# Feed-forward tiles of 512 columns in pairs whose matmuls take turns

## The chip, the cores and the metric

The kernel runs on one core of a Trainium2 chip. The metric is the device time in microseconds (us) of one execution. A core has a matrix engine (TensorE, in the profile PE for the matmuls and PEld for the loads of their stationary operand), a vector engine (VectorE, DVE), a scalar engine (ScalarE, ACT), GpSimd (POOL), and queues that issue DMAs (SyncE, SP). TensorE writes its results to PSUM, which has eight banks; one bank holds a tile of 128 partitions by 512 columns in float32. VectorE and ScalarE read the tiles from there.

## The reference

Attention with a sigmoid in the place of the softmax, for 8 batches of 12 heads, 448 positions and 64 channels, and on its output a gated feed-forward layer without bias:

```python
scores = scale * np.matmul(q, k.transpose(0, 1, 3, 2)) - np.log(S)
attn = 1.0 / (1.0 + np.exp(-scores))
attn_out = np.matmul(attn, v)                     # (8, 12, 448, 64)
x = attn_out.transpose(0, 2, 1, 3).reshape(3584, 768)
gate = 1.0 / (1.0 + np.exp(-(x @ w_gate)))        # 768 -> 1536
val = x @ w_val                                   # 768 -> 1536
out = gate * val @ w_out                          # 1536 -> 768
```

## The kernel before, in words

The attention part comes first and fills the first 258 us. Its matmuls (L225 and L244) are not touched. Then two feed-forward stages follow: gate and value in the first, the output projection in the second. Both compute transposed: output channels on the partitions, tokens along the columns.

The 3584 tokens are seven tiles of 512 columns. Six of them are taken in three sets of two (PAIR), and each such set is multiplied by a Strassen-like scheme with seven block products (`SETS`, index i from 0 to 6), with sums of weight blocks and of token blocks prepared beforehand. The seventh tile is the set ALONE, with four products. So a stage has the sets PAIR, ALONE, PAIR, PAIR, with 7, 4, 7 and 7 products; one product is called a round here.

Every float32 operand is split in two parts, a high one (the value rounded to the matmul's format) and a low one (the rest). A product of two blocks of 128 is three matmuls, low weight by high data, high by low, high by high, all added into one accumulator in PSUM. The function `product` (L403) issues them: for each of three blocks of the contraction three matmuls, nine in all, one after the other into the same accumulator `acc`. Each matmul has 128x128 weights and 512 columns, so an accumulator fills a bank.

**First stage** (loops at L469 to L560): three passes over the weights, in each the four sets, in each set its rounds r, and in each round four output tiles q, two of the gate and two of the value in turns (q even: gate, q odd: value). Per q: nine matmuls, then the reading of the accumulator (ScalarE copies for i = 0 and takes the sigmoid; VectorE adds or multiplies for the others), then `tick()` (L530), which issues what fell due (stores of results, splits of later weights), and then by q the splits of coming operands: `high_x` on ScalarE after q = 1, `low_x` on VectorE after q = 2 (with the load of a later operand), and steps that prepare the later weights on VectorE and GpSimd (L554 to L558).

**Second stage** (loops at L576 to L635): the same four sets and their rounds, in each round two halves of the contraction, and in each half three output tiles o. Per half and o again nine matmuls; an accumulator collects both halves and is read after the second (`evacuate`, L583). `high_h` and `low_h` split the coming operands, one per half.

`starts` (L400) says in which rounds a tile begins a new accumulator: rounds 0, 2 and 5 of PAIR, 0 and 2 of ALONE. `bank()` (L397) then hands out the next of the eight banks. In the other rounds the nine matmuls add onto what the same bank already holds, also where it has been read in between: such a tile is read after round 0 and added to in round 1, read after 2 and added to in 3, and so on.

The order of all work is written out by hand: each engine takes its instructions in the order in which the program issues them, and the framework adds the waits between engines, here above all that a matmul which adds to a bank waits for the read before it, and that a read waits for the last matmul before it.

Of the kernel before, what the change touches and what calls it, by code (L numbers as in the profile page):

```python
# [39 lines left out]
def sigmoid_attention_glu_kernel(ctx: ExitStack, tc: tile.TileContext, qk, v, wg, wv, wo, out):  # L40
    nc = tc.nc
# [8 lines left out]
    HC = NC // 2  # L50
# [5 lines left out]
    NQUAD = 2 * JS  # L56
# [22 lines left out]
    def tick(flush=False):  # L79
        clock[0] += 1  # L80
        due = [e for e in later if e[0] <= clock[0] or flush and e[2]]
        later[:] = [e for e in later if e not in due]
        for _, fn, _ in due:
            fn()

    def new_w(i):
        return keep.tile([P, NQUAD, 2, HW], F32R, tag=f"w{i}", name=f"w{i}")

    W = [new_w(i) for i in range(NP)]
# [79 lines left out]
    x_loaded, ops = {}, {}  # L169
# [25 lines left out]
    with tc.tile_pool(name="att", bufs=2) as att, tc.tile_pool(name="sc", bufs=2, space=PSUM) as scp, \  # L195
# [157 lines left out]
        for cols in (S, S // 2):  # L353
            for h in range(2):
                for u in range(2):
                    nc.tensor.matmul(sc[halves[u], h, :cols], lhsT=zeros[halves[h]], rhs=zeros[halves[h], :1].broadcast_to([HP, cols]),
                                     start=True, stop=True)
        beats, beat, done = B * NQ * 7, 0, 0
        for m in range(B * NQ):
            for g in range(7):  # L360
# [21 lines left out]
                if beats - 7 < beat < beats - 3:  # L382
                    k = beat - beats + 6
# [11 lines left out]
    with tc.tile_pool(name="mm", bufs=8, space=PSUM, reuse_waits="tile") as mm:  # L395

        def bank():  # L397
            return mm.tile([P, F], F32, tag="mm", name="acc")

        def starts(p, n):  # L400
            return n in (0, 2, 5) if SETS[p] is PAIR else n in (0, 2)

        def product(acc, pairs, first, half=None):  # L403
            terms = []
            for w, x, k in pairs:
                terms += [(w[:, 1, k[0]], x[:, 0, k[1]]), (w[:, 0, k[0]], x[:, 1, k[1]]), (w[:, 0, k[0]], x[:, 0, k[1]])]
            for n, (a, b) in enumerate(terms):
                nc.tensor.matmul(acc, lhsT=a, rhs=b, start=first and n == 0 and half != 1, stop=n == len(terms) - 1 and half != 0,  # L408
                                 skip_group_check=not first)

        def cols(k):
            return slice(k * P, (k + 1) * P)

        def add(o, a, b):
            nc.vector.tensor_tensor(out=o, in0=a, in1=b, op=ALU.add)  # L415
# [5 lines left out]
        o_order = [(p, k, h) for p in range(NSET) for _, k in SETS[p] for h in range(2)]  # L421
        h_loaded, h_ops, wx = {}, {}, {}

        def load_h(m):
            if m < len(o_order):
                p, i, h = o_order[m]
                h_loaded[m] = src_tile() if m < 4 or h == 0 else fo.tile([P, 3, F], F32, tag="src2", name="src2", bufs=2)
                nc.sync.dma_start(out=h_loaded[m], in_=h_src[p][i][h])

        def high_h(m):  # L430
            if m < len(o_order):
                h_ops[m] = op_tile() if m % 4 < 3 else fo.tile([P, 2, 3, F], F32R, tag="op2", name="op2", bufs=1)
                high(h_ops[m], h_loaded[m])

        def low_h(m):
            if m < len(o_order):
                low(h_ops[m], h_loaded.pop(m))
# [17 lines left out]
        with tc.tile_pool(name="ff", bufs=1, reuse_waits="tile") as ff:  # L455
# [6 lines left out]
            n = 0  # L462
# [6 lines left out]
            for s in range(NPASS):  # L469
                for p in range(NSET):  # L470
                    st = [{} for _ in range(NQUAD)]
# [3 lines left out]
                    for r, (i, _) in enumerate(SETS[p]):  # L475
                        for q in range(NQUAD):
                            d, t, jl = st[q], q % 2, q // 2
                            j = s * JS + jl
                            gate = st[q - 1] if t else None
                            if starts(p, r):  # L480
                                d["acc"] = bank()
                            acc = d["acc"]
                            product(acc, [(W[i][:, q], ops[n], (cols(k), k)) for k in range(HC)], starts(p, r))
                            if SETS[p] is ALONE:
                                if r % 2 == 0:
                                    pass
# [21 lines left out]
                            elif i in (2, 3):  # L508
                                k = "u2" if i == 2 else "u3"
                                d[k] = unit(k, 4)  # L510
                                add(d[k], acc, d["s1"])
                            else:
                                k, to = {4: ("s1", 1), 5: ("u3", 6), 6: ("u2", None)}[i]
# [55 lines left out]
        with tc.tile_pool(name="fo", bufs=1, reuse_waits="tile") as fo:  # L569
            def unit2(tag):  # L570
                return fo.tile([P, F], F32, tag=tag, name=tag, bufs=3)

            tick(flush=True)
            load_h(5)
            m = 0
            for p in range(NSET):  # L576
                st = [{} for _ in range(HC)]

                def save(o, b, y, queue=nc.sync, a=slice(0, F)):
                    t = (BLOCK[p] + b) * F  # L580
                    queue.dma_start(out=out[o, :, t + a.start:t + a.stop], in_=y[:, a])

                def evacuate(r, i, o, d, acc):  # L583
                    if SETS[p] is ALONE:
                        if r % 2:
                            y = unit2("c11" if r == 1 else "s1")
                            nc.scalar.copy(y, acc)
                            save(o + r // 2 * HC, 0, y)
                    elif i == 0:
                        d["s1"] = unit2("s1")  # L590
                        nc.scalar.copy(d["s1"], acc)
                    elif i == 1:
                        y = unit2("c11")
                        nc.scalar.copy(y, acc)
                        save(o, 0, y)
                    elif i in (2, 3):
                        k = "u2" if i == 2 else "u3"
                        d[k] = unit2(k)
                        add(d[k], acc, d["s1"])
                    else:  # L600
                        k, mo, b = {4: ("s1", HC, 0), 5: ("u3", HC, 1), 6: ("u2", 0, 1)}[i]
                        if m + 2 < len(o_order) or o < HC - 1:
                            add(d[k], acc, d[k])
                            save(o + mo, b, d[k])
                        else:
                            for queue, a in ((nc.scalar, slice(0, F // 2)), (nc.sync, slice(F // 2, F))):
                                add(d[k][:, a], acc[:, a], d[k][:, a])
                                save(o + mo, b, d[k], queue, a)

                for r, (i, _) in enumerate(SETS[p]):  # L610
                    for half in range(2):
                        for o in range(HC):
                            d = st[o]
                            if half == 0 and starts(p, r):
                                d["acc"] = bank()
                            js = range(3 * half, 3 * half + 3)
                            product(d["acc"], [(W[i][:, j] if j < NQUAD else wx[i][:, j - NQUAD], h_ops[m + half], (cols(o), j % 3)) for j in js], starts(p, r), half)
                            if half == 1:
                                evacuate(r, i, o, d, d["acc"])
                            tick()  # L620
                            if (half, o) == (0, 0) and m > 0:
                                high_h(m + 2)
                            if (half, o) == (0, 1) and m > 0:
                                low_h(m + 2)
                                load_h(m + 6)
                            if (half, o) == (1, 1):
                                high_h(m + 3)
                            if (half, o) == (1, 2):
                                low_h(m + 3)
                                load_h(m + 7 if m > 0 else 6)  # L630
                                if m == 0:
                                    load_h(7)
                    h_ops.pop(m)
                    h_ops.pop(m + 1)
                    m += 2  # L635
# [39 lines left out]
```

## Time and profile before

| | |
|---|---|
| runs | 1180.48, 1181.24, 1181.71 us (median 1181.24) |
| profiled execution | 1181.84 us, its span 1180.0 us |
| attention, by TensorE | up to 258.2 us |
| feed-forward stages, by TensorE | 918.26 us, 4050 matmuls |
| of these the first stage | 75 rounds of 36 matmuls |
| and the second | 25 rounds of 54 matmuls |
| granted TensorE clock | 1.000 |

The page gives the busy time of each engine, the span in 40 slices, the DMA queues, the chain of work that ended last, and the costliest groups of instructions. A row of the timeline has the start and the length in us from the span's start, the engine, the line, the operation, out<-in by tile names, shapes, and the number of instructions that were merged; in brackets stands the idle time of the engine before it and what ended that. A matmul's row is longer than the distance to the next one, since matmuls overlap. In the second stage weights with j below 4 are in a tile named w, the others in wr, wf or wsum.

### The profile page before, as it was taken

Reading aid. Unit: us, or ns where it says so; the run is one execution under the profiler, and the core shown is the slowest. Engines: PE = TensorE matmul, PEld = TensorE weight load, DVE = VectorE, ACT = ScalarE, POOL = GpSimd, SP = SyncE. Lnnn points to the kernel's source line nnn. Section 1 sums busy time; section 2 is a strip of 40 time slices with the busy share of each in tenths; the row PEclk is TensorE's granted clock in tenths of the full one; section 3 lists DMA queues with packets and bytes.
Section 4 is the critical chain, followed back from the end, with each engine's and each line's share of the span. In section 5 each row is a group of like instructions: output and inputs, shape, how many; then the busy total and the mean of one; then the engine's idle time right before and its main releaser. Section 6 shows DMA issues by size and latency. Waiting matters only on the chain.

```text
span 1180.0 us, 17018 instructions
## 1 busy us (share of the span) xinstructions
PE 1175.3 (100%) x6754; PEld 858.2 (73%) x6754; DVE 698.6 (59%) x725; ACT 488.6 (41%) x516; POOL 301.6 (26%) x232
## 2 busy tenths in 40 slices
PE   9999999999999999999999999999999999999998
PEld 3333333348888888888888888888888888888887
DVE  3334334326898658889965888657685542334343
ACT  6777777772232325322233532324344212422320
POOL 1325225161362413146340425405020000000000
PEclk9999999999999999999999999999999999999999
DMA  7588866867798576759967666746786453445531
GB/s 295 164 249 279 287 222 224 310 233 263 237 322 297 195 250 222 262 181 334 309 204 271 226 213 230 260 158 200 277 278 242 164 198 141 156 154 182 176 110 72
DMA packets 105520, 266.95 MB, mean 226 GB/s; under 512 B 19936, under 2 KB 54880, under 8 KB 105440
## 3 DMA queue, kind: packets, MB, share of 16 engines
q1 hardware_dynamic: 105296, 265.73, 65.8%
q8 instruction: 53, 0.87, 0.3%
q14 instruction: 27, 0.22, 0.1%
q10 hardware_dynamic: 144, 0.13, 0.0%
HBM read 178.91 MB, written 86.90 MB: 225 GB/s over the span
## 4 chain that ended last, share of the span: by engine, by line
PE 99%; DMA 0%; DVE 0%; DVEq 0%; issue 0%
PE acc L408 78%; PE sc L225 11%; PE av L244 11%; DMA qk<-qk 0%; PE av L225 0%; DVE u L415 0%; DVEq L669 0%
## 5 line engine op out<-in xcount | busy, mean ns | idle before, releaser
L408 PE MATMUL acc<-op,w 128*128 128x512 f32 x3600 | 828.3, 389 | 0.0
L408 PEld LDWEIGHTS acc<-op,w 128*128 128x128 f32 x3600 | 675.8, 188 | 140.8 <-issue 0.7
L181 DVE TENSOR_TENSOR op<-src,op 128x1536 fp32r<-128x1536 f32 x125 | 233.7, 1880 | 107.6 <-ACT op L178 57.4
L178 ACT CAST op<-src 128x1536 fp32r<-128x1536 f32 x124 | 183.1, 1479 | 188.8 <-PE acc L408 173.5
L228 ACT ACTIVATE a<-sc,bias 128x896 f32<-128x896 f32 x167 | 168.2, 1007 | 64.5 <-PE sc L225 60.7
L225 PE MATMUL sc<-qk 64*64 64x448 f32 x1336 | 155.5, 541 | 0.2 <-DMA qk<-qk 0.2
L244 PE MATMUL av<-a,v 64*64 64x448 f32 x1344 | 154.7, 536 | 0.0
L415 DVE TENSOR_TENSOR u<-acc,s 128x512 f32<-128x512 f32 x90 | 61.6, 687 | 76.5 <-PE acc L408 76.4
L225 PEld LDWEIGHTS sc<-qk 64*64 64x64 f32 x1336 | 48.3, 134 | 78.4 <-issue 65.7
L244 PEld LDWEIGHTS av<-a,v 64*64 64x64 f32 x1344 | 48.3, 133 | 78.1 <-issue 77.4
L527 POOL TENSOR_TENSOR t<-u,v 128x512 f32<-128x512 f32 x17 | 32.4, 1905 | 279.9 <-DVE u L418 230.2
L415 DVE TENSOR_TENSOR u<-acc,u 128x512 f32<-128x512 f32 (+1 forms) x91 | 61.7, 681 | 63.0 <-PE acc L408 62.8
L142 POOL TENSOR_TENSOR wsum<-wf 128x384 f32<-128x384 f32 x18 | 23.2, 1291 | 209.4 <-DVE wf L130 208.5
L520 ACT ACTIVATE u<-u 128x512 f32<-128x512 f32 x36 | 22.8, 633 | 92.0 <-DVE u L415 87.8
L520 ACT ACTIVATE s<-s 128x512 f32<-128x512 f32 x18 | 11.4, 632 | 102.5 <-DVE s L415 102.5
L415 DVE TENSOR_TENSOR s<-acc,s 128x512 f32<-128x512 f32 x45 | 31.0, 688 | 35.3 <-PE acc L408 35.2
L408 PE MATMUL acc<-op,wr 128*128 128x512 f32 x198 | 50.2, 389 | 0.0
L314 DVE TENSOR_TENSOR op<-av,op 128x448 f32<-128x448 f32 x24 | 15.0, 624 | 58.6 <-ACT op L268 58.6
L314 DVE TENSOR_TENSOR x<-av,x 128x448 f32<-128x448 f32 x24 | 15.0, 624 | 51.1 <-ACT x L268 50.8
L408 PEld LDWEIGHTS acc<-op,wr 128*128 128x128 f32 x198 | 37.2, 188 | 7.7
L130 DVE SCALAR_TENSOR_TENSOR wf<-wr,wf 128x768 uint32<-128x768 uint32 x36 | 41.9, 1164 | 0.7
L443 DVE TENSOR_TENSOR w<-w 128x1536 fp32r<-128x1536 f32 x21 | 41.1, 1959 | 0.0
(62 smaller groups left out, 709.0 us busy)
## 6 DMA issues: line engine op xcount, KB each, us to landing
src<-xs SPq DMA_DIRECT2D x75, 768.0 KB, 4.9
src<-hs SPq DMA_DIRECT2D x50, 768.0 KB, 5.3
qk<-qk SPq DMA_DIRECT2D x23, 896.0 KB, 5.0
hs<-t SPq DMA_DIRECT2D x78, 256.0 KB, 5.8
w<-ws SPq DMA_DIRECT2D x14, 768.0 KB, 6.6
v<-vv SPq DMA_DIRECT2D x23, 448.0 KB, 4.6
wr<-wg SPq DMA_DIRECT2D x12, 768.0 KB, 6.8
wr<-wv SPq DMA_DIRECT2D x12, 768.0 KB, 6.6
```

The costliest lines, as they stand in the source:

```text
L130: nc.vector.scalar_tensor_tensor(out=a, in0=raw[:, :, 0], scalar=29, in1=a, op0=ALU.logical_shift_right, op1=ALU.bitwise_or)
L178: nc.scalar.copy(op[:, 0], src)
L181: nc.vector.tensor_tensor(out=op[:, 1], in0=src, in1=op[:, 0].bitcast(F32), op=ALU.subtract)
L225: nc.tensor.matmul(sc[halves[u], h, :S], lhsT=qkt[halves[h], p, k0:k0 + HP], rhs=qkt[halves[h], p, :S], start=True, stop=True)
L228: nc.scalar.activation(a, sc[:, :, :S], AF.Sigmoid, bias=bias, scale=scale)
L244: nc.tensor.matmul(avs[key][halves[h], :S], lhsT=vt[halves[u], g, h], rhs=a[halves[u], h], start=start, stop=g == last)
L314: nc.vector.tensor_tensor(out=x, in0=other, in1=x, op=ALU.add)
L408: nc.tensor.matmul(acc, lhsT=a, rhs=b, start=first and n == 0 and half != 1, stop=n == len(terms) - 1 and half != 0, skip_group_check=not ...
L415: nc.vector.tensor_tensor(out=o, in0=a, in1=b, op=ALU.add)
L443: nc.vector.tensor_tensor(out=w[:, :, 1], in0=w[:, :, 1].bitcast(F32), in1=w[:, :, 0].bitcast(F32), op=ALU.subtract)
L520: nc.scalar.activation(d[k], d[k], AF.Sigmoid)
L527: nc.gpsimd.tensor_tensor(out=o, in0=a, in1=b, op=ALU.subtract)
```

## The change

`product`, which issues the matmuls of one tile, becomes `products`, which takes a list of tiles and issues the first matmul of each, then the second of each, and so on. In the first stage it is called at q = 0 and q = 2 with the tiles (q, q + 1), whose banks are taken there, and nothing is issued at q = 1 and q = 3. In the second stage the six groups of a round, numbered e = 3 half + o, are taken in the pairs (0, 1), (2, 3), (4, 5); the pair (2, 3) is half 0 of o = 2 with half 1 of o = 0. The very last round of the second stage keeps its order tile by tile. Reads of accumulators, ticks, splits, loads and stores stay where they were in the program.

```diff
-        def product(acc, pairs, first, half=None):
-            terms = []
-            for w, x, k in pairs:
-                terms += [(w[:, 1, k[0]], x[:, 0, k[1]]), (w[:, 0, k[0]], x[:, 1, k[1]]), (w[:, 0, k[0]], x[:, 0, k[1]])]
-            for n, (a, b) in enumerate(terms):
-                nc.tensor.matmul(acc, lhsT=a, rhs=b, start=first and n == 0 and half != 1, stop=n == len(terms) - 1 and half != 0,
-                                 skip_group_check=not first)
+        def products(tiles):
+
+            terms = [[] for _ in tiles]
+            for t, (_, pairs, _, _) in zip(terms, tiles):
+                for w, x, k in pairs:
+                    t += [(w[:, 1, k[0]], x[:, 0, k[1]]), (w[:, 0, k[0]], x[:, 1, k[1]]), (w[:, 0, k[0]], x[:, 0, k[1]])]
+            last = len(terms[0]) - 1
+            for n in range(last + 1):
+                for t, (acc, _, first, half) in zip(terms, tiles):
+                    nc.tensor.matmul(acc, lhsT=t[n][0], rhs=t[n][1], start=first and n == 0 and half != 1, stop=n == last and half != 0,
+                                     skip_group_check=not first)
...
-                            if starts(p, r):
-                                d["acc"] = bank()
+                            if q % 2 == 0:
+                                for w in (q, q + 1):
+                                    if starts(p, r):
+                                        st[w]["acc"] = bank()
+                                products([(st[w]["acc"], [(W[i][:, w], ops[n], (cols(k), k)) for k in range(HC)], starts(p, r), None) for w in (q, q + 1)])
                             acc = d["acc"]
-                            product(acc, [(W[i][:, q], ops[n], (cols(k), k)) for k in range(HC)], starts(p, r))
...
-                            if half == 0 and starts(p, r):
-                                d["acc"] = bank()
-                            js = range(3 * half, 3 * half + 3)
-                            product(d["acc"], [(W[i][:, j] if j < NQUAD else wx[i][:, j - NQUAD], h_ops[m + half], (cols(o), j % 3)) for j in js], starts(p, r), half)
+                            e = half * HC + o
+                            turn = (e,) if m + 2 == len(o_order) else (e, e + 1) if e % 2 == 0 else ()
+                            tiles = []
+                            for hh, oo in (divmod(w, HC) for w in turn):
+                                if hh == 0 and starts(p, r):
+                                    st[oo]["acc"] = bank()
+                                js = range(3 * hh, 3 * hh + 3)
+                                tiles.append((st[oo]["acc"], [(W[i][:, j] if j < NQUAD else wx[i][:, j - NQUAD], h_ops[m + hh], (cols(oo), j % 3)) for j in js], starts(p, r), hh))
+                            if tiles:
+                                products(tiles)
                             if half == 1:
                                 evacuate(r, i, o, d, d["acc"])
```

## The prediction

> **What bounds the kernel now.** I read the page's shares first, then the chain of waits, then who makes TensorE wait, and last single matmuls in the timeline.
>
> ```profile
> span 1180.0 us, 17018 instructions
> PE 1175.3 (100%) x6754; PEld 858.2 (73%) x6754; DVE 698.6 (59%) x725; ACT 488.6 (41%) x516; POOL 301.6 (26%) x232
> PE 99%; DMA 0%; DVE 0%; DVEq 0%; issue 0%
> ```
>
> The chain in order of time, its last pieces:
>
> ```profile
> 255.94 2.25 PE av L244 x24
> 258.20 918.26 PE acc L408 x4050
> ```
>
> The waits of TensorE over the whole span, longest first, and the matmul line with its duration (min/median/max):
>
> ```profile
> PE sc L356 <- DVE bias L66: 1.0, 1, 1.0
> PE sc L225 <- DMA qk<-qk: 0.2, 1, 0.2
> ...
> L408 PE MATMUL acc<-op,w x3600: 387/389/497, 258.1 to 1174.7; 128*128 128x512 f32 x190
> ```
>
> TensorE's own stream sets the end. The feed-forward matmuls, which the change reorders, are one unbroken piece: 4050 in 918.26 us, 226.7 ns from start to start, and none waits. So the change gains only if that step shrinks, and loses by every wait it lets into the stream. The profiled execution took 1181.84 us, 1.84 around its span; the median of the runs is 1181.24, so I add differences to that.
>
> **Does a change of bank shorten the step?** The kernel before already changes bank after every nine matmuls, so the trace holds the answer. In the output stage the timeline separates matmuls by their weight tile: in the second half of an output tile three read w, then six read wr, and the next w belongs to the next accumulator.
>
> ```profile
> 877.08 1.52 PE L408 MATMUL acc<-op,wr 128*128 128x512 f32 x6
> 878.44 0.84 PE L408 MATMUL acc<-op,w 128*128 128x512 f32 x3
> 879.12 1.52 PE L408 MATMUL acc<-op,wr 128*128 128x512 f32 x6
> 880.48 0.84 PE L408 MATMUL acc<-op,w 128*128 128x512 f32 x3
> ...
> 882.52 1.75 PE L408 MATMUL acc<-op,w 128*128 128x512 f32 x7
> 901.56 1.52 PE L408 MATMUL acc<-op,wr 128*128 128x512 f32 x6
> 902.92 0.84 PE L408 MATMUL acc<-op,w 128*128 128x512 f32 x3
> ...
> 907.00 6.96 PE L408 MATMUL acc<-op,w 128*128 128x512 f32 x30
> ```
>
> And the sixth wr matmul alone, the last write to its bank, from narrow windows of the same timeline:
>
> ```profile
> 878.21 0.39 PE L408 MATMUL acc<-op,wr 128*128 128x512 f32 x1
> 880.25 0.39 PE L408 MATMUL acc<-op,wr 128*128 128x512 f32 x1
> 882.29 0.39 PE L408 MATMUL acc<-op,wr 128*128 128x512 f32 x1
> 902.69 0.39 PE L408 MATMUL acc<-op,wr 128*128 128x512 f32 x1
> 906.77 0.39 PE L408 MATMUL acc<-op,wr 128*128 128x512 f32 x1
> ```
>
> Inside a bank five steps take 878.21 - 877.08 = 1.13 us, 0.226 each. Across a bank 878.44 - 878.21 = 0.23, and 0.23 in the other four pairs too (880.48, 882.52, 902.92, 907.00). Had each bank change saved 10 ns, these would read 0.22 or 0.21. I take the gain per turn as nothing; the rows' rounding leaves some 3 ns either way, which I keep for the rival.
>
> The Trainium skill, "TensorE: Matmul & The Clock Gate", section "Back-to-back issue gap", gives N/2.4 + 2.5 ns for a warm matmul: an estimated 215.8 ns at 512 columns, so by that page this stream has 10.9 ns too much in every step. Were that excess the price of staying in one bank, the some 3550 steps that newly change bank would save an estimated 39 us; the trace disagrees with the figure (226.7), and its bank changes cost the same 0.23.
>
> **What the turns move in the first feed-forward stage.** No matmul, weight load or DMA is added or removed, and the program order on ScalarE, VectorE, GpSimd and the queues stays. What moves is when an accumulator is finished and when its bank is written again. Number the matmuls of a round (one i) from 0. Before, tile q owns 9q to 9q+8. After, tiles 0 and 1 share 0 to 17 and end at 16 and 17; tiles 2 and 3 end at 34 and 35. So tiles 0 and 2 are read 8 steps, 1.81 us, later. Where the next round accumulates into the same bank, its first write used to come 28 steps after the last one; now it comes 20 steps after. A reader has about 4.3 us, less its own latency, where it had 6.1. Ahead of tile 3's read VectorE has tile 2's read, the 1.75 us split of an operand (L181), and in some rounds a weight step. The tightest case is the round that starts at 568.3 (258.13, first row below, + 38 rounds of 36 x 0.2267), where VectorE runs behind:
>
> ```profile
> 258.13 4.17 PE L408 MATMUL acc<-op,w 128*128 128x512 f32 x17
> ...
> 572.78 0.68 DVE L415 TENSOR_TENSOR u<-acc,s 128x512 f32<-128x512 f32 x1
> 573.38 0.94 DVE L128 SCALAR_TENSOR_TENSOR wf<-wr,wf 128x768 uint32<-128x768 uint32 x1
> 574.24 1.28 DVE L415 TENSOR_TENSOR u<-acc,s 128x512 f32<-128x512 f32 x2
> 575.44 1.75 DVE L181 TENSOR_TENSOR op<-src,op 128x1536 fp32r<-128x1536 f32 x1
> 577.11 0.95 DVE L130 SCALAR_TENSOR_TENSOR wf<-wr,wf 128x768 uint32<-128x768 uint32 x1
> 577.98 1.48 DVE L415 TENSOR_TENSOR u<-acc,s 128x512 f32<-128x512 f32 x2
> ```
>
> After the change tile 2 is finished by matmul 34 (576.06); a reader starts 0.43 later (measured below), so 576.49 to 577.17; by the row-to-row steps L181 follows to 578.84, L130 to 579.70, tile 3's read from 579.62 to 580.30. Tile 3 is written again by matmul 55 counted from this round's start, whose weights load as 54 starts, at 580.59. So 0.27 us is left and TensorE does not wait; without a weight step about 1.1 us is left. Cost taken: nothing. If VectorE's split stretched, as it did at the stage's start (second row below, 2.61 for 1.75), some three rounds as tight as this one would lose up to 0.6 us each, 1.8 in all.
>
> ```profile
> 258.84 0.62 DVE L314 TENSOR_TENSOR x<-av,x 128x448 f32<-128x448 f32 x1 [2.18 <-ACT x L268]
> ...
> 260.22 2.61 DVE L181 TENSOR_TENSOR op<-src,op 128x1536 fp32r<-128x1536 f32 x1 [0.75 <-ACT op L178]
> ```
>
> The very first pair writes its second bank 8 steps earlier, at 258.35 instead of 260.17, while the attention's last tiles are still being read. The first accumulator starts at 258.13 under the same reads, so I take nothing; the bound is the 1.1 us until VectorE's last such read ends, 258.84 + 0.62 in the row above.
>
> **What the turns move in the output stage: here a wait comes in.** A round has 54 matmuls, six groups of nine: half 0 of o = 0, 1, 2, then half 1. The pairs are (half 0: o 0, o 1), (half 0: o 2; half 1: o 0), (half 1: o 1, o 2). So o = 1 ends at matmul 52, and the next round's first pair begins with o = 0 at 54 and o = 1 at 55. Before, o = 1 ended at 44 and was next written at 63. Where the next round accumulates into the bank that `evacuate` has just to read, matmul 55 must wait for that read. The reads and their start after the last write:
>
> ```profile
> 903.12 0.69 DVE L415 TENSOR_TENSOR u<-acc,s 128x512 f32<-128x512 f32 x1 [4.39 <-PE acc L408]
> 905.16 0.69 DVE L415 TENSOR_TENSOR u<-acc,s 128x512 f32<-128x512 f32 x1 [1.35 <-PE acc L408]
> 905.77 1.75 DVE L443 TENSOR_TENSOR w<-w 128x1536 fp32r<-128x1536 f32 x1
> 907.44 0.68 DVE L415 TENSOR_TENSOR u<-acc,s 128x512 f32<-128x512 f32 x1
> 908.04 3.41 DVE L181 TENSOR_TENSOR op<-src,op 128x1536 fp32r<-128x1536 f32 x2
> ...
> 880.73 0.59 ACT L591 COPY s<-acc 128x512 f32<-128x512 f32 x1 [1.50 <-PE acc L408]
> ```
>
> The weight loads of the same stretch, and a release from VectorE to another engine:
>
> ```profile
> 878.22 0.64 PEld L408 LDWEIGHTS acc<-op,w 128*128 128x128 f32 x3
> ...
> 301.93 0.68 DVE L415 TENSOR_TENSOR u<-acc,u 128x512 f32<-128x512 f32 x1
> 302.64 0.63 ACT L520 ACTIVATE u<-u 128x512 f32<-128x512 f32 x1 [3.03 <-DVE u L415]
> ```
>
> A read starts 903.12 - 902.69 = 0.43 us after its last matmul starts; VectorE then needs 0.69, ScalarE 0.59; the next engine starts 302.64 - 302.61 = 0.03 later; a weight load leads its matmul by 878.44 - 878.22 = 0.22. For the round that ends at 907.00: matmul 52 starts at 906.54, VectorE reads from 906.97 to 907.66, releases at 907.69. Matmul 55 is due at 907.23, its weight load at 907.01. Held at the weight load, the stream slips 907.69 - 907.01 = 0.68 us; with ScalarE as reader 0.58. Nothing stands ahead of these reads: both engines sat idle before them (1.35, 1.50).
>
> Where the release finds the weights already loaded, only the matmul waits: 0.46 and 0.36. The Trainium skill, "TensorE: Matmul & The Clock Gate", section "Step-by-step: what each phase is for", has weight loads pulled ahead of matmuls in flight, and by that rule it would be these smaller figures. In the trace a load runs one matmul ahead and no further; I take the larger.
>
> How often: a PAIR set reads and goes on accumulating at four joints of rounds: 0 to 1 (ScalarE), 2 to 3, 3 to 4 and 5 to 6 (VectorE). ALONE has none, as its banks are read only in rounds after which new banks start. Three PAIR sets make 12; the very last round runs tile by tile, so o = 1 comes back only at matmul 63 there, which leaves 11: 3 by ScalarE, 8 by VectorE. Sum: 8 x 0.68 + 3 x 0.58 = 7.2 us; with the weights ahead 8 x 0.46 + 3 x 0.36 = 4.8. If a halted stream restarts as slowly as its first matmul (497 ns against 389), 11 x 0.11 = 1.2 more.
>
> The second operand half is needed at matmul 19 of a round instead of 27. Its low part follows both reads and, in five rounds by the code's delays, L443: by the rows 906.97, + 0.61, + 1.67, + 0.60, + 1.75 = 911.60, against a need at 907.00 + 20 x 0.2267 + 0.68 of slip = 912.2. It fits; where no slip precedes it lacks about 0.1 us, once. The end of the kernel is the unchanged single-tile round.
>
> Sum: 0 (banks) + 0 (first stage) + 7.2 + 0.1: **1181.2 + 7.3 = 1188.5 us**, 0.6% slower.
>
> **Rivals.** *The bank matters after all*, by something these bank changes do not show, such as an effect of a whole stream that alternates. It decides from 7.3 us / 3550 = 2 ns per step; at 10 ns it gives 1188.5 - 35.5 = 1153. For it: the step's 226.7 is not explained. Against it: five changes at 0.23. Chance 4%. *The wait does not bite*: the readers finish in time or matmul 55 goes ahead, 1181.3 us. Against it: a read of 0.69 us stands in a gap of three steps, 0.68, and starts 0.43 into it. Chance 8%. *VectorE becomes late in the first stage too*: 1188.5 + 1.8, and with the slow restart 1191.5. For it: 0.27 us of slack in a busy round; against it: 1.1 in the plain ones. Chance 10%. The forecast keeps 78%.
>
> **Range.** From the low side of the waits, 1181.2 + 4.8 = 1186, one lower for the runs' spread (1180.48 to 1181.71), to 1188.5 + 1.8 + 1.2 and 0.5 of the spread, 1192. What lies outside is the first two rivals and little more. A measurement of this kernel tells about 0.2%, 2.4 us: slower 0.88, same 0.08, faster 0.04.
>
> **What would show it.** In the profile after: TensorE's waits list VectorE's L415 (eight) and ScalarE's copies (three) with 0.5 to 0.7 us each, all in the output stage at the start of a round; the step inside stays 0.227; the first stage shows no wait. A step near 0.216, or no such waits, makes the forecast wrong; waits between 260 and 870 us make the third rival right.

## The result

The kernel after takes 1189.39 us (median; 1188.19 to 1189.80) against 1180.86 of the kernel before: 1.0068 of it, with a 95% interval of 1.0055 to 1.0080. It is slower by 0.7%; 1188.5 was forecast, in a range of 1185 to 1192. The 1180.86 is the median of four runs; the longer series of the kernel before beside the experiments have 1181.15 to 1181.57. The profiled execution took 1189.41 us with a span of 1187.6.

The page of the kernel after, its span, shares and chain (line 412 is now the matmul line, L419 the adding read of an accumulator, L597 ScalarE's copying one, L447 the split of later weights on VectorE):

```profile
span 1187.6 us, 17017 instructions
PE 1179.1 (99%) x6754; PEld 856.8 (72%) x6754; DVE 696.9 (59%) x725; ACT 485.0 (41%) x516; POOL 303.6 (26%) x232
...
PE 92%; issue 4%; DMA 1%; DVE 1%; POOL 1%; POOLq 0%; SPq 0%; ACT 0%; DVEq 0%; ACTq 0%
```

The same instructions do the same work; but the chain, which was TensorE for 99%, now leaves TensorE and comes back. (The 4% of "issue" are mostly one piece of 44.5 us from 826.44, where the chain goes from a halt back over VectorE, a DMA and GpSimd; TensorE was busy for 44.26 us of it, so it is no loss of that size.) Its last pieces in order of time (start, length, number of matmuls) show where:

```profile
888.53 19.81 PE acc L412 x86
909.11 12.10 PE acc L412 x52
921.98 24.38 PE acc L412 x106
947.13 73.30 PE acc L412 x322
1021.13 24.34 PE acc L412 x106
1046.24 12.10 PE acc L412 x52
1059.11 24.34 PE acc L412 x106
1084.22 24.34 PE acc L412 x106
1109.22 24.36 PE acc L412 x106
1134.35 12.10 PE acc L412 x52
1147.21 36.84 PE acc L412 x161
```

What was one piece of 4050 matmuls is cut at the joints of rounds: 52 is a round of 54 less two, 106 two rounds less two. Who was waited for, first by the matmuls and then by the weight loads (us in total, times, longest):

```profile
PE acc L412 <- DVE u L419: 2.9, 9, 0.3
...
PE acc L412 <- ACT s L597: 0.8, 3, 0.3
```

```profile
PEld acc L412 <- DVE u L419: 6.4, 9, 0.8
...
PEld acc L412 <- ACT s L597: 2.0, 3, 0.7
PEld acc L412 <- issue: 1.3, 2, 0.7
...
PEld acc L412 <- DVE op L181: 0.6, 2, 0.5
```

The kernel before had only the issue row for its feed-forward loads, 0.7 once. Three waits on ScalarE's copies are there, and nine on VectorE's reads: eight are the forecast joints, the ninth lies in the first stage, near 862 us, right behind the second of the issue rows (0.6 us): two halts in a row. One joint close up, the round that ends near 908.4 (timeline; in brackets the idle time ahead):

```profile
908.17 0.19 PEld L412 LDWEIGHTS acc<-op,w 128*128 128x128 f32 x1
908.37 0.69 DVE L419 TENSOR_TENSOR u<-acc,s 128x512 f32<-128x512 f32 x1 [3.16 <-PE acc L412]
908.39 0.39 PE L412 MATMUL acc<-op,w 128*128 128x512 f32 x1
...
908.97 1.75 DVE L447 TENSOR_TENSOR w<-w 128x1536 fp32r<-128x1536 f32 x1
909.11 3.50 PEld L412 LDWEIGHTS acc<-op,w 128*128 128x128 f32 x16 [0.75 <-DVE u L419]
909.11 3.70 PE L412 MATMUL acc<-op,w 128*128 128x512 f32 x15 [0.33 <-DVE u L419]
```

Matmul 54 goes at 908.39, and with it the weight load of 55 was due. VectorE's read of o = 1 ends at 908.37 + 0.69 = 909.06, and the load starts at 909.11.

Did the turns shorten the step? Matmuls within 500 us of the first stage, from the windows view of the kernel before and then of the kernel after:

```profile
300.00:800.00 500.00, 500.00 (x2207) 414.17 (x2206) 394.51 (x394) 163.42 (x172) 178.69 (x106) 1.00 0.71 245
```

```profile
300.00:800.00 500.00, 500.00 (x2208) 414.29 (x2207) 393.05 (x393) 161.03 (x172) 179.33 (x106) 1.00 0.71 244
```

2207 matmuls with a bank change at one step in nine, 2208 with a bank change at every step (inside a pair, and from one pair to the next). One count is the edge of a window; the step is 226.7 ns in both. A bank that changes is worth nothing here.

### The profile page after: what moved, and what is told of

Its sections match the earlier page's. It is cut to its first block, busy times and chain, and to the rows that moved or that the text cites. A ratio compares the mean times of both kernels' runs of the same rounds, so it can differ in the third digit from the quotient of the medians.

```text
span 1187.6 us, 17017 instructions
## 1 busy us (share of the span) xinstructions
PE 1179.1 (99%) x6754; PEld 856.8 (72%) x6754; DVE 696.9 (59%) x725; ACT 485.0 (41%) x516; POOL 303.6 (26%) x232
## 4 chain that ended last, share of the span: by engine, by line
PE 92%; issue 4%; DMA 1%; DVE 1%; POOL 1%; POOLq 0%; SPq 0%; ACT 0%; DVEq 0%; ACTq 0%
PE acc L412 71%; PE sc L225 11%; PE av L244 11%; DMA hs<-t 1%; DVE u L419 1%; POOL t L533 1%; DVE op L181 0%; DMA qk<-qk 0%; POOLq L681 0%; DVE w L447 0%; ACT s L597 0%; SPq L464 0%; PE av L225 0%; SPq L450 0%; DVEq L681 0%
## 5 line engine op out<-in xcount | busy, mean ns | idle before, releaser
L412 PE MATMUL acc<-op,w 128*128 128x512 f32 x3600 | 848.2, 390 | 3.7 <-DVE u L419 2.9
L181 DVE TENSOR_TENSOR op<-src,op 128x1536 fp32r<-128x1536 f32 x125 | 235.8, 1897 | 109.0 <-ACT op L178 106.9
L419 DVE TENSOR_TENSOR u<-acc,s 128x512 f32<-128x512 f32 x90 | 60.3, 686 | 86.8 <-PE acc L412 86.8
L419 DVE TENSOR_TENSOR u<-acc,u 128x512 f32<-128x512 f32 (+1 forms) x91 | 60.0, 680 | 64.8 <-PE acc L412 64.7
L412 PE MATMUL acc<-op,wr 128*128 128x512 f32 x198 | 57.4, 390 | 0.0
L419 DVE TENSOR_TENSOR s<-acc,s 128x512 f32<-128x512 f32 x45 | 30.0, 686 | 34.9 <-PE acc L412 34.8
L447 DVE TENSOR_TENSOR w<-w 128x1536 fp32r<-128x1536 f32 x21 | 41.1, 1958 | 0.0
```

The lines of the kernel that those rows point to most:

```text
L181: nc.vector.tensor_tensor(out=op[:, 1], in0=src, in1=op[:, 0].bitcast(F32), op=ALU.subtract)
L412: nc.tensor.matmul(acc, lhsT=t[n][0], rhs=t[n][1], start=first and n == 0 and half != 1, stop=n == last and half != 0, skip_group_check=no ...
L447: nc.vector.tensor_tensor(out=w[:, :, 1], in0=w[:, :, 1].bitcast(F32), in1=w[:, :, 0].bitcast(F32), op=ALU.subtract)
```

## The experiments

All times stand against the kernel before, run beside them: 1181.57 us for the first four experiments, 1181.15 for the others but one, where it is given. A slip is the time by which a halt sets the matmul stream back. It is worked out from the matmuls' starts in the trace: the halted step and the next one, less two steps of 0.227 (for the two halts in a row near 862 us four steps, less four).

**The change in the first stage alone.**

```diff
-turn = (e,) if m + 2 == len(o_order) else (e, e + 1) if e % 2 == 0 else ()
+turn = (e,)
```

> The change in the first stage alone; the output stage runs tile by tile as before. Wait theory (the loss is the wait of matmul 55 for the read of o = 1, in the output stage): about 0.8 us over before, all of it the one halt that the changed kernel's trace shows at 862 us, where VectorE reads two tiles late; 1181.7. Rival (taking turns itself costs, spread over all steps of both stages): two thirds of the 8 us, since two thirds of the matmuls lie here: 1186.

Measured: 1181.88 us against 1181.57, ratio 1.0005 (0.9996 to 1.0015). In its trace the output stage has no halt, and the first stage has the one near 862, 0.76 us. The loss does not come from taking turns as such.

**The change in the output stage alone** (the first stage calls `products` with one tile at a time).

```diff
-if q % 2 == 0:
-    for w in (q, q + 1):
-        ...
-    products([... for w in (q, q + 1)])
+if starts(p, r):
+    d["acc"] = bank()
+products([(d["acc"], [(W[i][:, q], ops[n], (cols(k), k)) for k in range(HC)], starts(p, r), None)])
```

> The change in the output stage alone. Wait theory: 11 halts of 0.54 (after ScalarE) and 0.60 us (after VectorE), 6.4 together, one more of 0.3 us for the low part of an operand and some 0.3 that the trace leaves unplaced: 7.1 us over before, 1188.0. Rival (turns cost per step): one third of the 8 us, 1183.6.

Measured: 1188.63 us, ratio 1.0058 (1.0043 to 1.0073), 7.1 us more. The waits of its weight loads:

```profile
PEld acc L412 <- DVE u L419: 6.0, 8, 0.8
...
PEld acc L412 <- ACT s L595: 2.0, 3, 0.7
...
PEld acc L412 <- issue: 0.7, 1, 0.7
...
PEld acc L412 <- DVE op L181: 0.2, 1, 0.2
```

Eight and three, the joints counted ahead of the run. The further halt of 0.3 us for the low part of an operand did not come: of such waits only one is left, 0.15 us of a weight load, which sets the stream back by 0.05. In the trace the matmul stream is 6.8 us longer than before: 6.4 in the eleven halts, 0.4 in the steps behind them (see the sum below). A third of the matmuls carries nearly all of the loss.

**The bank needed one step sooner.** The output stage alone again, with o = 1 ahead of o = 0 in the first pair of a round.

```diff
-turn = ... else (e, e + 1) if e % 2 == 0 else ()
+turn = ... else (e + 1, e) if e == 0 else (e, e + 1) if e % 2 == 0 else ()
```

> Output stage alone, pairs as in the change, but in the first pair of a round o = 1 goes ahead of o = 0, so its bank is written again at matmul 54, one step sooner. Wait theory: each of the 11 halts grows by one step, 0.227 us: 2.5 us more than with the change in the output stage alone, 1190.5. Rival (turns cost per step): no difference from the run with the change in the output stage alone.

Measured: 1191.03 us, ratio 1.0082 (1.0065 to 1.0098), 2.4 us over the run before it, where 2.5 was expected; the matmul streams of the two traces differ by 2.8 us. The joint that was shown above, in this run (TensorE sat idle for 0.33 us there, for 0.65 here):

```profile
907.72 4.57 PE L412 MATMUL acc<-op,w 128*128 128x512 f32 x19 [0.65 <-DVE u L419]
```

A halt after ScalarE slips 0.77 us in place of 0.54, one after VectorE 0.89 in place of 0.60: a step or a little more each. No matmul, pair or count of turns differs between the two; only the distance from a bank's last write to its next one does, so the wait for the read is the cause.

**The bank needed later.** The output stage alone, o = 0 by itself, o = 1 and o = 2 in turns.

```diff
-turn = ... m + 2 == len(o_order) else (e, e + 1) if e % 2 == 0 else ()
+turn = ... m + 2 == len(o_order) or e % 3 == 0 else (e, e + 1) if e % 3 == 1 else ()
```

> Output stage alone, other pairs: in each half o = 0 runs alone and o = 1 takes turns with o = 2, so two thirds of the steps of the stage still take turns, but o = 1 ends at matmul 52 and is next written at 63 instead of 55. Wait theory: no halt, TensorE waits for nothing, time of before, 1180.9 within 0.5. Rival (turns cost per step, whatever the distance): two thirds of what the output stage loses in the run with the change there alone, about 4.7 us over before.

Measured: 1184.39 us, ratio 1.0024 (1.0015 to 1.0034). Neither expectation holds: 2.8 us over before, where the one said 0 and the other 4.7. The waits and one of the joints in its timeline:

```profile
PEld acc L412 <- DVE u L419: 2.0, 2, 1.0
PEld acc L412 <- ACT s L595: 1.5, 3, 0.5
```

```profile
907.39 0.69 DVE L419 TENSOR_TENSOR u<-acc,s 128x512 f32<-128x512 f32 x1 [3.16 <-PE acc L412]
...
908.00 1.75 DVE L447 TENSOR_TENSOR w<-w 128x1536 fp32r<-128x1536 f32 x1
909.66 0.69 DVE L419 TENSOR_TENSOR u<-acc,s 128x512 f32<-128x512 f32 x1
...
910.40 3.73 PEld L412 LDWEIGHTS acc<-op,w 128*128 128x128 f32 x17 [0.98 <-DVE u L419]
```

The halt of o = 1 is gone. But o = 2 ends right after o = 1 and is now needed at matmul 10 of the next round, and its read stands behind a weight split on VectorE (0.61 after the first read began, then 1.66), in three other rounds behind ScalarE's 1.48 us operand split. Five halts slip 0.83 twice, 0.36 twice and 0.31 once, 2.7 us together. I had reckoned the distance of one tile and not looked at what is queued ahead of the other's read.

**The two weight splits put off.** The first stage alone, with two splits due four ticks later.

```diff
-fetch_w(wx[i], o_src[i][:, NQUAD:])
+fetch_w(wx[i], o_src[i][:, NQUAD:], 14 if i == 6 else 10)
...
-... (10, 10, 20, 22, 24, 26, 28)[i])
+... (10, 14, 20, 22, 24, 26, 28)[i])
```

> The change in the first stage alone, and the splits of two weight tiles (L440 on ScalarE, L443 on VectorE by the lines of before), which fall due in round 4 of the last set, are put off by four ticks into round 5. Theory (the one halt of the first stage comes from VectorE's reads of tiles 0 and 1 in round 5 standing behind 2.7 us of such splits and a late operand split): the halt at 862 us shrinks from 0.78 us to below 0.2. Rival (the halt is the end of the stage's order, whatever the splits): it stays at about 0.8. In the time, 1181.7 against 1180.9, hardly to be told; the trace decides.

Measured: 1181.20 us, ratio 1.0003 (0.9993 to 1.0012). The halt near 862 is gone altogether; in the trace the mean step of the first stage is 226.68 ns, that of the kernel before to the hundredth. In the changed kernel the stretch on VectorE reads thus:

```profile
855.73 1.76 DVE L181 TENSOR_TENSOR op<-src,op 128x1536 fp32r<-128x1536 f32 x1 [1.43 <-ACT op L178]
857.40 0.69 DVE L419 TENSOR_TENSOR s<-acc,s 128x512 f32<-128x512 f32 x1
858.19 0.69 DVE L422 TENSOR_TENSOR s<-s,s 128x512 f32<-128x512 f32 x1
858.80 1.75 DVE L447 TENSOR_TENSOR w<-w 128x1536 fp32r<-128x1536 f32 x1
860.47 0.95 DVE L447 TENSOR_TENSOR wsum<-wsum 128x768 fp32r<-128x768 f32 x1
861.34 1.28 DVE L419 TENSOR_TENSOR u<-acc,u 128x512 f32<-128x512 f32 x2
```

VectorE waits 1.43 us for an operand from ScalarE and then has two weight splits ahead of the two reads, which end at 861.34 + 1.28 = 862.62. The matmuls that write to these two banks again were due from 861.79 and halt twice:

```profile
862.17 4.20 PE L412 MATMUL acc<-op,w 128*128 128x512 f32 x16 [0.21 <-DVE u L419]
...
862.67 3.50 PEld L412 LDWEIGHTS acc<-op,w 128*128 128x128 f32 x16 [0.35 <-DVE u L419]
```

The kernel before has the same stretch, with the same wait and the same splits, but there the two reads end at 861.13, a microsecond ahead of the first matmul that needs their banks (862.12):

```profile
859.85 1.28 DVE L415 TENSOR_TENSOR u<-acc,u 128x512 f32<-128x512 f32 x2
```

So the change did not put the splits there; it moved the whole stretch back. The reads start 1.49 us later in a trace whose matmul stream starts 0.35 us earlier; the 1.84 us are about the 8 steps (1.81) by which the change ends tiles 0 and 2 later. With the splits put off the reads start at 857.10:

```profile
857.10 1.29 DVE L419 TENSOR_TENSOR u<-acc,u 128x512 f32<-128x512 f32 x2 [0.33 <-PE acc L412]
```

**Turns in both stages, the known waits avoided:** the splits put off and the output stage as in the run with the bank needed later (whose pairing is taken here to be free of halts).

> Turns in both stages with both kinds of halt designed away: the first stage in pairs with the splits put off, the output stage with o = 0 alone and o = 1, o = 2 in turns. Nearly nine in ten of the steps change bank. If a change of bank is worth nothing: the time of before, 1180.9 within 1. If it is worth something that the waits of the change had covered: 3500 steps at 1 ns each would already be 3.5 us, 1177.

Measured: 1184.10 us, ratio 1.0023 (1.0015 to 1.0032), with the same five halts at matmul 10. So it could not yet say what the turns alone are worth.

**The same with both reads first.** In the second half the reads of o = 1 and o = 2 are issued together.

```diff
 if half == 1:
-    evacuate(r, i, o, d, d["acc"])
+    for oo in (o,) if len(turn) == 1 else (o, o + 1) if turn else ():
+        evacuate(r, i, oo, st[oo], st[oo]["acc"])
```

> As the run with turns in both stages and o = 0 alone, but the reads of o = 1 and o = 2 in the second half are issued back to back, before the tick and the operand split that stood between them. Wait theory (the 2.8 us left in the two runs with o = 1 and o = 2 in turns are five halts of matmul 10 for the read of o = 2, which stands behind a weight split of 1.75 us on VectorE in two of them and behind an operand split of 1.48 us on ScalarE in three): no halt is left, 1181 within 1. Rival (turns cost some 2.8 us in the output stage by themselves): 1184 again. If a change of bank is worth something: below 1180.

Measured: 1181.09 us against 1181.20, ratio 1.0000 (0.9991 to 1.0009). The feed-forward matmuls are one piece again, as long as in the kernel before:

```profile
258.04 918.26 PE acc L412 x4050
```

All of the first stage and two thirds of the output stage (but its last round) take turns here, nothing halts, and the piece takes 918.26 us, to the hundredth what it took with nine matmuls in a row to one bank. This settles both: the loss was the waits, and the turns are worth nothing. No run beat the kernel before.

**What the step consists of.** In the kernel before, all but the first of a tile's nine matmuls in the first stage cover only the first columns of the set's width; the columns left out miss those terms.

```diff
+part = slice(0, width if n else F)
-nc.tensor.matmul(acc, lhsT=a, rhs=b, ...)
+nc.tensor.matmul(acc[:, part], lhsT=a, rhs=b[:, part], ...)
```

> What sets the step of 226.7 ns. The kernel before; in the first stage all but the first of the nine matmuls of a tile cover only the first 512, 448, 384 and 256 columns in the sets 0 to 3, so the other columns of these accumulators miss terms and the output is not the reference's. Streaming theory (512 columns at one rate plus a fixed part): steps of 226.7, 200.0, 173.4 and 120. Weight-load theory (a load of 188 ns plus a fixed 39 sets the step): 226.7 in all four sets. Mixed: falls with the width down to a floor near 190 to 200 and stays there.

Runs of matmuls of one width, from narrow windows of the timeline (start, length, count; the last one's own length is 0.28, 0.33 and 0.37):

```profile
410.26 1.00 PE L409 MATMUL acc<-op,w 128*128 128x256 f32 x7
```

```profile
380.36 1.20 PE L409 MATMUL acc<-op,w 128*128 128x384 f32 x6
```

```profile
341.17 1.60 PE L409 MATMUL acc<-op,w 128*128 128x448 f32 x7
```

(1.00 - 0.28) / 6 = 0.120 us at 256 columns, (1.20 - 0.33) / 5 = 0.174 at 384, (1.60 - 0.37) / 6 = 0.205 at 448, and 0.2267 at 512. Three of the four lie where the streaming theory had them. 448 is 5 ns above; over the whole run its steps spread from 199 to 207 ns, and why is open. From 256 to 512 columns a step grows by 106.7 ns, 0.417 ns a column, which leaves 226.7 - 213.4 = 13.3 ns a matmul. The weight load theory falls: at 256 columns a step is shorter than a load of 188 ns, so loads overlap each other, as the loads of the same stretch show, (0.79 - 0.19) / 5 = 0.12 us from start to start:

```profile
410.38 0.79 PEld L409 LDWEIGHTS acc<-op,w 128*128 128x128 f32 x6
```

The whole run took 1118.88 us once, with 34.8 us of matmuls waiting for VectorE's reads, so narrower steps turn the reads into a bound. Its time is not one of full clock throughout: in seven stretches of 3.4 to 6.8 us the granted clock was 0.50 (0.983 over the run). The rows above lie outside them, at 1.00.

## Why the prediction was right

**The bank changes.** Taken at nothing, from five changes at 0.23 us. Right: 918.26 us with and without turns once no wait is left. (A single pair of rows leaves up to 10 ns by rounding, more than the 3 kept; the matmuls' starts in the trace of before put every step of the output stage, bank changes included, at 225 to 228 ns.) The 215.8 ns estimated by the rule of the Trainium skill ("TensorE: Matmul & The Clock Gate", "Back-to-back issue gap") are not what these float32 matmuls reach: the widths put 13.3 ns, not 2.5, on top of 0.417 ns a column, and the bank has no part in it. Where the 13.3 come from no run here shows.

**The wait in the output stage.** Right in place, number and releasers: 11 halts at matmul 55, three by ScalarE, eight by VectorE. The size of one was forecast a little high: it is 0.60 in place of 0.68 after VectorE, 0.54 (once 0.49) in place of 0.58 after ScalarE; together 6.4 us of the 7.2. What was mis-sized is the restart. The load was later than reckoned, 909.11 - 908.39 = 0.72 us after it was due, in part because the release took 0.05 and not 0.03. But in the trace the halted matmul then begins with its load and not 0.22 behind it, while the next one follows after 0.335 us, 0.11 more than a step: 0.72 - 0.22 + 0.11 gives the 0.60, to rounding. The 0.11 is the slow restart that the prediction kept for its range and not for its sum; that the lead of the load falls away it did not see. The smaller figures, 0.46 and 0.36, for weights loaded ahead, were wrong: the loads stand in the trace as the waiting instructions.

**The operand half needed sooner.** The 0.1 us where no slip precedes came once, as 0.05, in the sixth round. "It fits" was wrong in another: at matmul 21 of the second round, behind a slip of 0.54, the stream slips 0.35 us more for L181. In the trace VectorE's subtraction ahead of it (L574) waits for a DMA of results until 884.45:

```profile
884.45 0.69 DVE L574 TENSOR_TENSOR t<-s,t 128x512 f32<-128x512 f32 x1 [4.78 <-DMA hs<-t]
...
888.53 0.76 PEld L412 LDWEIGHTS acc<-op,w 128*128 128x128 f32 x4 [0.49 <-DVE op L181]
```

Before, it waited only until 883.01:

```profile
883.01 0.69 DVE L568 TENSOR_TENSOR t<-s,t 128x512 f32<-128x512 f32 x1 [4.61 <-DMA hs<-t]
```

I had worked out the rounds with L443 alone and left that wait out. With the change in the output stage alone the subtraction starts at 883.14, and there this halt is absent; why the DMA landed later in the one profile is open.

**The first stage.** Taken at nothing; 0.78 us was lost, in a round other than the one I worked out as the tightest. By the sign that the prediction itself had named, a wait between 260 and 870 us, the third rival, to which it gave 10%, held in this: VectorE is late in the first stage, within the bound of 1.8, but not by a stretched split. It is late by a wait for ScalarE and two weight splits ahead of the reads, as the run with the splits put off shows; these stand in the trace of before, at a place that I had not worked out.

**The sum.** 6.4 + 0.35 + 0.78 = 7.5 us of the 7.9 by which the matmul stream is longer. The other 0.4 are in the unhalted steps of the output stage, 226.97 ns in place of 226.67 on average (226.96 with the change there alone, 226.69 with no halts). The matmuls' starts show where: each halt is followed by four to eight steps of 229 to 241 ns (behind the joint at 909.11 they are 231, 235, 229, 232 and 231), and the sixth round has seven such steps where an operand came 0.05 us late. In the rounds of this stage without a wait every step is 225 to 228 ns. Why a halt leaves such a tail is open. In the medians the loss is 8.5 us (7.8 to 8.2 against the longer series of the kernel before), against 7.3 forecast; the profiled spans differ by 7.6. That the sum came this near is in part luck: the waits at the joints were forecast 0.8 us too high, and some 1.4 us of other losses were left out.

## What to carry to other kernels

Reordering a stream that never waits can only lose unless a step gets shorter, and whether it can is often already in the trace: look for the places where the present order does what the new one would do everywhere. When matmuls of several tiles take turns, each tile ends later and is wanted again sooner; count the steps from the last write of a bank to its next, and set against them the read with everything queued ahead of it on its engine. Where such a distance has become short, issuing the reads first and letting the tile that ended first come back first cost nothing here.

## What was not expected of the hardware

The step of these matmuls follows the columns at 0.417 ns each plus 13.3 ns (120, 174 and 227 ns at 256, 384 and 512; 448 is off at 205), also where it falls below the 188 ns of a weight load. A halted stream pays less than the delay of its weight load, 0.60 of 0.72 us. And a halt does not end with the wait: the next step takes 0.335 us and some four to eight more 229 to 241 ns, before they are 226.7 again.
